# Two-layer mixture kernel: preparing the second layer's factors by a model of the queues, Strassen sums held in PSUM, a plain last w2 product

## The chip, the cores and the metric

The kernel runs on one core of a Trainium2 chip. The metric is device time in microseconds (us), from one launch to its end. TensorE multiplies matrices, VectorE, ScalarE and GpSimd work element by element, SyncE (SP) issues DMAs; each works through its own queue in order and waits there on semaphores. In the profile's rows PE is TensorE, PEld its weight loads, DVE is VectorE, ACT is ScalarE and POOL is GpSimd. Ln is line n of the kernel before.

## The reference

```python
# chunked attention (4 x 8 heads, 576 positions, chunks of 64, 64 wide) gives x, 2304 x 512
scores = scale * np.matmul(q_c, k_c.transpose(0, 1, 2, 4, 3))
...
x = np.ascontiguousarray(attn_out.transpose(0, 2, 1, 3)).reshape(B * S, H * D)
# layer 1: w_a, w_b 512 x 1536, w_out 1536 x 512
a = x @ w_a
b = x @ w_b
x = (a * b @ w_out).astype(np.float32)
# layer 2: 4 experts, w1 512 x 1024, w2 1024 x 512
p = domain_probs / (domain_probs.sum(-1, keepdims=True) + 1e-09)
for e in range(E):
    h = np.maximum(x @ w1[e], 0.0)
    out += p[:, e:e + 1] * (h @ w2[e])
```

## The kernel before, in words

**Numbers and products.** All is computed near float32. A factor is split into a rounded high half (fp32r) and the rest (low half): split_hi is a ScalarE cast (L96), sub_hi a subtraction, on GpSimd by default (L111). A product of two factors is three matmuls (high by high, high by low, low by high) into one PSUM bank of 512 columns; a weight tile is 128x128. add is a VectorE tensor_tensor (L99), add_sb a VectorE scalar_tensor_tensor (L103).

**Strassen.** Tokens come in blocks: block 0 has 256, blocks 1 to 4 have 512 each. From the third of six groups of layer 1 weights (F) on, blocks 1 and 2 are done together by seven half-size products in place of eight, in seq (L621 inside half_mm issues the matmuls; the name A marks this step in the loops). ScalarE copies the first bank (L646), and VectorE forms the four results in SBUF tiles. In layer 2 blocks 1 and 2 (first pass, p = 0) and blocks 3 and 4 (second pass, p = 1) go through the same seq for w1 and through seven products for w2.

**Layer 1.** Attention runs in slots between matmul groups, densest at the start. ab_steps (L508) makes a and b of one block; end_b multiplies them on VectorE, and to_parts splits the product into gh (high) and ag (low, GpSimd). x2_steps (mm3, L461 to L463) multiplies them by w_out and adds into xacc on VectorE, some steps later; the list after says behind which step. The 36 w1 tiles come as float64 and are converted by prep_begin (L140 to L154) and split by prep_end and ent_s, at places written out by hand (put).

**Preparation of the second layer's factors.** prep_ahead is a list of closures that prep takes one by one at fixed steps. A unit is half of one of 16 groups of w1 and w2, one 512 KB raw tile: 32 units. For each there are two split halves, four 256-column Strassen sums in place on VectorE (sums, L103), two more halves, and for each of the four a 512 KB store to DRAM (save, from ScalarE's queue). The tile is loaded from SP's queue (L192) two units ahead. 87 of the 128 halves are made in layer 1, in weight tiles (w), and 41 in layer 2, in tiles of the raw pool (made).

**Layer 2.** The loop over s has 32 steps of w1 (a_steps, group a = s) interleaved, product by product, with the w2 products of the step before (o_step, o = s - 1, L852). a_steps runs seq; on weighs each result by relu and the expert's probability on VectorE (L810) and splits it (part_of_h). t_steps forms the four differences T1 to T4 on GpSimd (L832) and splits them. o_step's seven products go to pairs of PSUM banks (po, two pairs), and VectorE adds each into its y (L99, 1024 columns; ScalarE copies in a pass's first step, L859). In the first pass block 0 rides along: a0_step (24 matmuls of 256 columns) and o0_step (12 matmuls, L926). load_l2 loads the prepared weights from DRAM on SP, in an order written out once. ends forms the four outputs of a pass from the seven y's, on VectorE, 1024 columns each. In the last step t_steps runs on VectorE, and the seven products, ends and the stores follow each other.

Of the kernel before, what the change touches and what calls it, by code (L numbers as in the profile page):

```python
# [22 lines left out]

H_SCALE = 2.0**-112
H_MAX = (1.0 + 0x6FFFFF / 2.0**23) * 2.0**-96


@with_exitstack
def fused_kernel(
# [25 lines left out]
    nc = tc.nc  # L55
# [16 lines left out]
    w_p = ctx.enter_context(tc.tile_pool(name="w", bufs=9))  # L72
    raw_p = ctx.enter_context(tc.tile_pool(name="raw", bufs=4))
# [11 lines left out]
    def psum():  # L85
        return ps_p.tile([P, 512], F32, tag="ps", name="ps")

    def psum_m():
        return psm_p.tile([P, 512], F32, tag="pm", name="pm")
# [72 lines left out]

    def split_w(src, t=None, eng=nc.gpsimd):
# [6 lines left out]
    unsaved = []  # L170

    def save(behind=0):
        while len(unsaved) > behind:
            key, t = unsaved.pop(0)
            saved[key] = tc.dram_tile([P, 2, 512], F32, name="kept" + "_".join(map(str, key)))
            nc.scalar.dma_start(out=saved[key], in_=t.bitcast(F32))
# [5 lines left out]
    def prep_ahead():  # L182

        raw2 = {}
        todo = [(g, i) for g in range(NG2) for i in range(2)]

        def load(n):
            if n < len(todo):
                g, i = todo[n]
                r = raw2[n] = raw_p.tile([P, 1024], F32, tag="raw", name="raw2")  # L190
                src = w2p[g, :, 2 * i : 2 * i + 2, :]
                nc.sync.dma_start(out=r, in_=src.rearrange("p a n -> p (a n)"))  # L192

        def ent(n, k):
            g, i = todo[n]
            save()
            half = raw2[n][:, 512 * (k % 2) :][:, :512]
            t = None
            if "2" in late:
                t = raw_p.tile([P, 2, 512], F32R, tag="raw", name="made")  # L200
            t = split_w(half, t)
            unsaved.append(((g, 4 * i + k), t))
            if k == 3:
                load(n + 2)

        def sums(n):
            q = [raw2[n][:, 256 * x : 256 * x + 256] for x in range(4)]
            a11, a12, a22, a21 = q if todo[n][1] == 0 else (q[0], q[2], q[3], q[1])
            add_sb(a22, a21, a22)
            add_sb(a21, a11, a21, ALU.subtract)  # L210
            add_sb(a11, a22, a11, ALU.subtract)
            add_sb(a12, a12, a11, ALU.subtract)

        yield lambda: (load(0), load(1))
        for n in range(len(todo) + 1):
            if n < len(todo):
                yield from (lambda n=n, k=k: ent(n, k) for k in range(2))
            if n:
                yield from (lambda n=n, k=k: ent(n - 1, k) for k in (2, 3))
            if n < len(todo):  # L220
                yield lambda n=n: sums(n)

    ahead = list(prep_ahead())

    def prep(n=1):
        for _ in range(n):
            if ahead:
                ahead.pop(0)()

    wl = {}  # L230
    l2_loads = [(0, 0, n) for n in (0, 2, 3, 1)]
    for go in range(2 * NG2):
        for n in (0, 4, 2, 7, 5, 3, 6, 1):
            at = divmod(go + (n < 4), NG2)
            if at[0] < 2:
                l2_loads.append((*at, n))

    def load_l2(n=1):
        for _ in range(n):
            if l2_loads:  # L240
                p, g, k = l2_loads.pop(0)
                t = w_tile()
# [247 lines left out]
    def to_parts(g, h, l):  # L490
        split_hi(h, g)
        sub_hi(nc.gpsimd, l, g, h)

    def ab_steps(f, j, i0, nt):
# [21 lines left out]
        def end_b():  # L516
            g = st["g"][:, :n]
            add(g, st[1][:, :n], g, ALU.mult)
            gs[f, j, i0] = (gh_any()[:, :n], ag_tile(F32R)[:, :n])
            to_parts(g, *gs[f, j, i0])  # L520
# [33 lines left out]
    def combos(b11, b21, b12, b22, t_at, eng_b=nc.gpsimd, eng_t=nc.vector):  # L554
# [38 lines left out]
        s3 = [sub(t4, t2, b21)]  # L593
# [36 lines left out]
    def seq(w, t, on, bank=psum_m):  # L630
# [31 lines left out]
        add(t["c22"], pd, t["u3"])  # L662
        out("22", t["c22"])
# [8 lines left out]
        add(t["c12"], pd, t["u2"])  # L672
        flush()
        out("12", t["c12"])
# [68 lines left out]
    def seq_ab(F):  # L743
# [4 lines left out]
        def on_a(name, ap):  # L748
            if name == "11":
                nc.scalar.copy(out=ga["11"], in_=ap)  # L750

        def on_b(name, ap):
            g = ga[name]
            (add if name == "11" else add_sb)(g, ap, g, ALU.mult)
            f, j = 2 * F + (name[0] == "2"), int(name[1])
            gs[f, j, 0] = (gh_tile(name), ag_tile(F32R))
            to_parts(g, *gs[f, j, 0])

        def gen():
# [3 lines left out]
            t |= {"c22": t["m1"], "c12": t["u2"]}  # L763
            yield from seq(lambda x: left(F, 0, x), t, on_a, psum)
            t["m1"] = t["c22"] = gh_tile("22", F32)
            t["u2"] = t["c12"] = gh_tile("12", F32)
# [5 lines left out]

    H = {}
    G = {}
# [5 lines left out]
        ("A12", "B21"),  # L780
        ("S1", "T1"),
        ("S3", "T3"),
        ("S2", "T2"),
# [8 lines left out]
    def part_of_h(a, name, src, eng=nc.gpsimd):  # L792
        pool = late["1" if name in ("B11", "B22") else "2"]
        t = pool.tile([P, 2, 512], F32R, tag="h" + name, name="h" + name, bufs=1)
        H[a, name] = (t[:, 0, :], t[:, 1, :])
        split_hi(t[:, 0, :], src)
        sub_hi(eng, t[:, 1, :], src, t[:, 0, :])

    def a_steps(a):
# [3 lines left out]
        t = {n: late["1"].tile([P, 512], F32, tag=n, name=n, bufs=2) for n in ("m1", "u2", "u3", "g")}  # L803
        t["c22"], t["c12"] = t["m1"], t["u2"]
        prob = pb[p, g // GPE]

        def on(name, src):
            dst = t["g"] if name == "11" else src
            j = int(name[1]) - 1
# [8 lines left out]
            G[a, name] = dst  # L818
            if name != "12":
                part_of_h(a, "B" + name, dst)  # L820

        return steps_of(seq(lambda x: w[x], t, on), 7)

    def t_steps(a, eng):

        g11, g21, g12, g22 = (G[a, n] for n in ("11", "21", "12", "22"))

        def sub(o, x, y):
            if eng is nc.vector:
                add_sb(o, x, y, ALU.subtract)  # L830
            else:
                eng.tensor_tensor(out=o, in0=x, in1=y, op=ALU.subtract)  # L832

        return [
            lambda: (sub(g11, g12, g11), sub(g12, g22, g12)),
            lambda: (part_of_h(a, "T1", g11), sub(g22, g22, g11)),
            lambda: (part_of_h(a, "T3", g12), sub(g21, g22, g21)),
            lambda: part_of_h(a, "T2", g22),
            lambda: part_of_h(a, "T4", g21),
        ]  # L840

    def o_step(o, k, after=None):
# [4 lines left out]
        bh, bl = H.pop((o, part))  # L847
        ps = late["ps"].tile([P, 2, 512], F32, tag="po", name="po")
# [7 lines left out]
        if after is not None:  # L856
            add(y, y, ps, ALU.subtract)
        elif g == 0:
# [9 lines left out]
    def ends(p):  # L868
# [3 lines left out]
        def go(o, x, z, op=ALU.add, at=None):  # L872
            add_sb(y[o], y[x], y[z], op)
            if at:
# [9 lines left out]
            lambda: go("A22", "S3", "A22", ALU.subtract),  # L884
# [439 lines left out]
```

## Time and profile before

| | |
|---|---|
| median of 3 runs | 1315.87 us (1309.72 to 1317.66) |
| the profiled execution | 1309.49 us |
| its span, first to last instruction | 1307.7 us |
| mean granted TensorE clock | 0.979 |
| busy: TensorE, VectorE, GpSimd, ScalarE | 1230.7, 993.0, 889.2, 432.2 us |

A group of rows names a line, an engine, an operation, its tiles as out<-in, and its shapes; behind the bar are the idle time of the engine just before those instructions and what ended it. A row of waits reads: who waited, for whom, microseconds in total, times, longest. Matmuls are pipelined, so the end of a matmul row lies some 0.2 us after the start of the next one.

### The profile page before, as it was taken

The numbers are of one execution on the slowest core, as the hardware profiler recorded it, in microseconds if no ns is written. First come the engines' busy times: TensorE is split into PE (matmuls) and PEld (weight loads), VectorE is DVE, ScalarE is ACT, GpSimd is POOL, SyncE is SP. The second block draws the span as 40 slices with busy tenths as digits, with TensorE's granted clock in tenths as the row PEclk, the third lists the DMA queues.
The fourth block names the chain that finished last, engine by engine and source line by source line (L and its number), as shares of the span: only waits on it lengthen the run. The fifth ranks groups of instructions, "written<-read, shape, count | busy, mean of one in ns | idle before, by whom it ended". The sixth has DMA issues, their size and how long they took to land.

```text
span 1307.7 us, 18028 instructions
## 1 busy us (share of the span) xinstructions
PE 1230.7 (94%) x6674; PEld 1004.6 (77%) x6676; DVE 993.0 (76%) x1247; ACT 432.2 (33%) x785; POOL 889.2 (68%) x669
## 2 busy tenths in 40 slices
PE   8998899889899897999999999999999999999996
PEld 5876678668677776888887878788877888888884
DVE  7856458878686877755888788867788788778778
ACT  4644434433424333334222322222233222222221
POOL 4536567776656756656867776866787777777773
PEclk9999889899899998999999999999999999999998
DMA  8645434444435434266778767855537776676662
GB/s 283 220 138 189 176 130 165 156 161 150 173 128 179 160 129 145 113 221 239 264 253 285 276 248 273 290 176 189 183 129 271 254 247 219 211 246 225 207 213 79
DMA packets 76820, 261.35 MB, mean 200 GB/s; under 512 B 8546, under 2 KB 8618, under 8 KB 76732
## 3 DMA queue, kind: packets, MB, share of 16 engines
q1 hardware_dynamic: 58300, 193.07, 45.0%
q10 hardware_dynamic: 18432, 67.12, 12.7%
q8 instruction: 53, 0.87, 0.3%
q14 instruction: 35, 0.29, 0.1%
HBM read 188.29 MB, written 71.86 MB: 199 GB/s over the span
## 4 chain that ended last, share of the span: by engine, by line
PE 48%; DVE 15%; POOL 3%; issue 2%; ACT 2%; DMA 1%; DVEq 0%; ACTq 0%; POOLq 0%
PE pm L621 19%; PE po L852 18%; PE po L926 3%; DVE raw L103 3%; DVE y L99 3%; PE pm L508 2%; DVE u L810 2%; POOL w L111 1%; DMA raw<-in_w2p_dram 1%; PE ps L461 1%; PE ps L463 1%; PE ps L462 1%; DVE u L99 1%; PE pm L463 1%; PE pm L462 1%
## 5 line engine op out<-in xcount | busy, mean ns | idle before, releaser
L99 DVE TENSOR_TENSOR y<-po,y 128x1024 f32<-128x1024 f32 x209 | 253.8, 1219 | 69.4 <-PE po L852 69.2
L852 PE MATMUL po<-hT,w 128*128 128x512 f32 x768 | 197.8, 393 | 6.1 <-POOL hT L111 4.2
L621 PE MATMUL pm<-cT,w 128*128 128x512 f32 x768 | 195.9, 390 | 0.0
L621 PE MATMUL pm<-cB,w 128*128 128x512 f32 x672 | 175.1, 396 | 15.6 <-ACT ag L646 15.5
L852 PEld LDWEIGHTS po<-hT,w 128*128 128x128 f32 x768 | 144.6, 189 | 39.3 <-POOL hT L111 5.9
L111 POOL TENSOR_TENSOR w<-raw,w 128x512 fp32r<-128x512 f32 x87 | 121.8, 1400 | 77.1 <-ACT w L96 71.8
L621 PEld LDWEIGHTS pm<-cT,w 128*128 128x128 f32 x768 | 143.1, 188 | 29.9
L621 PEld LDWEIGHTS pm<-cB,w 128*128 128x128 f32 x672 | 126.0, 190 | 44.1 <-ACT ag L646 17.2
L852 PE MATMUL po<-hB,w 128*128 128x512 f32 x576 | 150.3, 397 | 7.9 <-DVE y L99 7.4
L852 PEld LDWEIGHTS po<-hB,w 128*128 128x128 f32 x576 | 106.8, 188 | 38.2 <-DVE y L99 14.5
L508 PE MATMUL pm<-xh,w 128*128 128x512 f32 (+1 forms) x576 | 135.8, 357 | 0.0
L103 DVE SCALAR_TENSOR_TENSOR raw<-raw 128x256 f32<-128x256 f32 x128 | 113.2, 885 | 12.2 <-POOL w L111 8.9
L461 PE MATMUL ps<-ag,w 128*128 128x512 f32 (+1 forms) x244 | 95.2, 390 | 23.2 <-POOL ag L111 21.2
L508 PEld LDWEIGHTS pm<-xh,w 128*128 128x128 f32 x576 | 99.7, 190 | 16.6
L111 POOL TENSOR_TENSOR ag<-ag,gh 128x512 fp32r<-128x512 f32 (+1 forms) x61 | 77.2, 1271 | 51.4 <-ACT gh L96 50.0
L99 DVE TENSOR_TENSOR xacc<-ps,xacc 128x512 f32<-128x512 f32 (+1 forms) x112 | 68.0, 628 | 40.8 <-PE ps L463 40.4
L96 ACT CAST w<-raw 128x512 fp32r<-128x512 f32 x87 | 53.9, 620 | 130.7 <-DMA raw<-in_w2p_dram 57.3
L111 POOL TENSOR_TENSOR hT<-u,hT 128x512 fp32r<-128x512 f32 x64 | 94.9, 1483 | 0.0
L463 PE MATMUL ps<-gh,w 128*128 128x512 f32 (+1 forms) x244 | 92.0, 377 | 0.5 <-POOL w L111 0.5
L154 POOL TENSOR_TENSOR t<-t,raw 128x512 int32<-128x512 int32 x36 | 47.5, 1319 | 66.1 <-issue 23.8
L462 PE MATMUL ps<-gh,w 128*128 128x512 f32 (+1 forms) x244 | 92.0, 377 | 0.0
L832 POOL TENSOR_TENSOR u<-m,u 128x512 f32<-128x512 f32 x62 | 82.6, 1331 | 2.4
(141 smaller groups left out, 2342.5 us busy)
## 6 DMA issues: line engine op xcount, KB each, us to landing
w<-kept SPq DMA_DIRECT2D x256, 512.0 KB, 4.6
kept<-w ACTq DMA_DIRECT2D x87, 512.0 KB, 2.6
kept<-made ACTq DMA_DIRECT2D x41, 512.0 KB, 5.9
raw<-in_w1p_dram SPq DMA_DIRECT2D x36, 512.0 KB, 3.7
raw<-in_w2p_dram SPq DMA_DIRECT2D x32, 512.0 KB, 4.5
q<-in_q_dram SPq DMA_DIRECT2D x18, 256.0 KB, 3.8
k<-in_k_dram SPq DMA_DIRECT2D x18, 256.0 KB, 4.2
v<-in_v_dram SPq DMA_DIRECT2D x18, 256.0 KB, 4.1
```

The lines of the kernel that those rows point to most:

```text
L96: nc.scalar.copy(out=dst, in_=src)
L99: nc.vector.tensor_tensor(out=out, in0=in0, in1=in1, op=op)
L103: nc.vector.scalar_tensor_tensor(out=out, in0=in0, scalar=1.0, in1=in1, op0=ALU.mult, op1=op)
L111: eng.tensor_tensor(out=dst, in0=src, in1=hi.bitcast(F32), op=ALU.subtract)
L154: nc.gpsimd.tensor_tensor(out=t.bitcast(I32), in0=t.bitcast(I32), in1=low.bitcast(I32), op=ALU.add)
L461: nc.tensor.matmul(out=ps[:, :n], lhsT=wh, rhs=al, start=(m == 0), stop=False)
L462: nc.tensor.matmul(out=ps[:, :n], lhsT=wh, rhs=ah, start=False, stop=False)
L463: nc.tensor.matmul(out=ps[:, :n], lhsT=wl, rhs=ah, start=False, stop=(m == last))
L508: nc.tensor.matmul(out=st[i][:, :n], lhsT=x, rhs=y, start=m == 0, stop=m == 3 * KD - 1)
L621: nc.tensor.matmul(out=ps, lhsT=x, rhs=y, start=first and kk == 0 and m == 0, stop=kk == 1 and m == 2, skip_group_check=not first,)
L832: eng.tensor_tensor(out=o, in0=x, in1=y, op=ALU.subtract)
L852: nc.tensor.matmul(out=ps[:, d, :], lhsT=x[:, s], rhs=y, start=m == 0, stop=m == 2)
```

## The change

1. Class Plan wraps the program builder: at build time it keeps, for each engine, the time at which its queue would be free, by a duration for each kind of instruction and by when each tile was written and last read. Nothing of it runs on the chip.
2. prep_ahead, prep and save go. prepare turns each unit into Jobs (a load from ScalarE's queue, four casts, four low halves and four sums on GpSimd, four stores); tick, called after most steps, issues those whose engine has room and whose inputs are due by the model, and first the jobs of rank 0 (the layer's own h parts). A unit is begun every 20 us of the model's TensorE time in layer 1, from the fourth span on, and every 14 in layer 2. load_l2 issues what is missing of a tile that it is asked for.
3. Pools: w 9 to 7 tiles plus 3 for made; raw 4 to 2 plus one raw2. load_l2's order of tiles changes.
4. to_parts subtracts on VectorE, and the product stays in its PSUM bank. seq takes A12 B21 sixth, not third, and leaves its results in PSUM. The x2 steps of layer 1 come at steps 6, 8 and 8 on (before 6, 8, 4, 5 and 8).
5. a_steps no longer uses seq: one bank takes four products, and T1 and T3 are formed on VectorE, T2 and T4 on GpSimd. PRODUCTS has a new order; the splits of h are Jobs.
6. The last step's w2 product is four plain products (o_last, 48 matmuls) added to y's on which ends(1) has been run before.

```diff
+class Plan:
...
+    def note(self, name, op, out, ins):
+        t = self.start(name, op, out, ins)
+        if op == "dma_start":
+            self.at[name] = t + 0.36
+            end = t + DMA_US
+        else:
+            us, port = self.cost(name, op, out, ins)
+            end = t + us
...
-    w_p = ctx.enter_context(tc.tile_pool(name="w", bufs=9))
-    raw_p = ctx.enter_context(tc.tile_pool(name="raw", bufs=4))
+    w_p = ctx.enter_context(tc.tile_pool(name="w", bufs=7))
+    raw_p = ctx.enter_context(tc.tile_pool(name="raw", bufs=2))
...
+        if SUMS == "DVE":
+            add_sb(o, y, z, op)
+        else:
+            nc.gpsimd.tensor_tensor(out=o, in0=y, in1=z, op=op)
...
+        def fits(self, now):
+            if not (self.when() and all(j.done for j in self.after)):
+                return False
+            free = max(plan.at[self.q], plan.at["port"] if self.q != "ACT" else 0)
+            if free > now + SLACK[self.rank][self.q] + (hurry() if self.rank else 0):
+                return False
+            return self.ready() <= max(free, now) + EARLY[self.q]
...
     def to_parts(g, h, l):
         split_hi(h, g)
-        sub_hi(nc.gpsimd, l, g, h)
+        add(l, g, h.bitcast(F32), ALU.subtract)
...
-            add(g, st[1][:, :n], g, ALU.mult)
+            b = st[1][:, :n]
+            add(b, b, g, ALU.mult)
...
-        half_mm(pa, w("A12"), c["B21"], first=False)
-        out("11", pa)
-        yield
         pc = psum_m()
         half_mm(pc, w("S3"), c["T3"])
-        flush()
         add(t["u3"], pc, t["u2"])
         yield
         pd = psum_m()
         half_mm(pd, w("S1"), c["T1"])
-        add(t["c22"], pd, t["u3"])
-        out("22", t["c22"])
+        add(pc, pd, t["u3"])
+        out("22", pc)
         yield
         pe = bank()
         half_mm(pe, w("A22"), c["T4"])
-        add(t["u3"], t["u3"], pe, ALU.subtract)
+        add(pe, t["u3"], pe, ALU.subtract)
         flush()
-        out("21", t["u3"])
+        out("21", pe)
+        yield
+        half_mm(pa, w("A12"), c["B21"], first=False)
+        flush()
+        out("11", pa)
...
+            x = psum_m()
+            half_mm(x, w["A11"], c["B11"])
+            nc.scalar.copy(out=t["m1"], in_=x)
+            yield
+            y = psum_m()
+            half_mm(y, w["S1"], c["T1"])
+            nc.scalar.copy(out=t["m5"], in_=y)
+            yield
+            half_mm(x, w["S2"], c["T2"], first=False)
+            nc.scalar.copy(out=t["u2"], in_=x)
+            yield
+            z = psum_m()
+            half_mm(z, w["A12"], c["B21"])
+            add(z, z, t["m1"])
+            weigh(t["g"], z, 0)
+            yield
+            part_of_h(a, "B11", t["g"])
+            half_mm(x, w["S3"], c["T3"], first=False)
+            v = psum_m()
+            add(v, x, t["m5"])
+            weigh(t["m5"], v, 1)
+            yield
+            part_of_h(a, "B22", t["m5"])
+            half_mm(y, w["S4"], c["B22"], first=False)
+            add(y, y, t["u2"])
+            weigh(y, y, 1)
+            yield
+            half_mm(x, w["A22"], c["T4"], first=False)
...
+            add(t["u2"], y, t["g"], ALU.subtract)
+            made_h[a, "B11"].run()
+            add(t["g"], t["m5"], y, ALU.subtract)
+            weigh(t["m1"], x, 0)
...
+                for k in (3, 4, 5, 6):
+                    e[k]()
+                for i, j in ((0, 1), (1, 1), (0, 0), (1, 0)):
+                    o_last(i, j)
+                break
```

## Rows read from the trace of the kernel before

**Rows 1.** The page, first part: busy time, share of the span, instructions.
```profile
PE 1230.7 (94%) x6674; PEld 1004.6 (77%) x6676; DVE 993.0 (76%) x1247; ACT 432.2 (33%) x785; POOL 889.2 (68%) x669
```

**Rows 2.** Windows: length, then busy (instructions) PE PEld DVE ACT POOL, PEclk, DMA.
```profile
75.00:570.00 495.00, 450.03 (x2340) 364.63 (x2339) 352.06 (x475) 192.83 (x346) 317.46 (x233) 0.96 0.44 156
592.86:851.09 258.23, 251.88 (x1201) 207.78 (x1201) 209.94 (x235) 77.56 (x146) 196.18 (x152) 1.00 0.75 265
851.09:950.35 99.26, 99.26 (x482) 83.58 (x481) 74.83 (x81) 22.26 (x42) 68.93 (x50) 1.00 0.54 180
950.35:976.70 26.35, 25.07 (x121) 20.72 (x121) 22.31 (x23) 10.03 (x15) 21.23 (x14) 1.00 0.47 160
979.32:1021.78 42.46, 39.27 (x170) 31.31 (x168) 35.12 (x33) 15.06 (x21) 33.80 (x21) 1.00 0.78 271
1059.67:1078.84 19.17, 19.17 (x85) 15.77 (x84) 15.15 (x16) 4.54 (x8) 14.43 (x11) 1.00 0.73 246
```

**Rows 3.** Waits of TensorE from 75 to 570 us, the four largest.
```profile
PE ps L461 <- POOL ag L111: 20.1, 12, 6.0
PE pm L621 <- ACT ag L646: 15.5, 4, 6.8
PE pm L621 <- DVE gh L99: 3.2, 3, 1.4
PE ps L621 <- DVE xacc L99: 2.6, 3, 1.6
```

**Rows 4.** Windows again: two of layer 1's seven half-clock stretches, and all seven summed.
```profile
344.41:351.23 6.82, 3.80 (x9) 3.02 (x10) 2.42 (x5) 3.25 (x6) 4.97 (x4) 0.50 0.26 107
494.60:501.42 6.82, 3.99 (x9) 3.14 (x10) 4.53 (x8) 3.53 (x7) 2.64 (x4) 0.50 0.21 85
sum 40.92, PE 30.69 PEld 24.37 DVE 21.55 ACT 13.59 POOL 26.14; mean PE 4.38 PEld 3.48 DVE 3.08 ACT 1.94 POOL 3.73
```

**Rows 5.** Timeline, 480 to 500 us: start, length, instruction, [idle before <-releaser].
```profile
484.94 0.62 ACT L96 CAST w<-raw 128x512 fp32r<-128x512 f32 x1 [6.99 <-DMA raw<-in_w2p_dram]
...
497.43 2.93 PE L621 MATMUL pm<-cB,w 128*128 128x512 f32 x6 [6.83 <-ACT ag L646]
```

**Rows 6.** Groups of instructions, shapes apart: busy us, mean ns | idle before.
```profile
L111 POOL TENSOR_TENSOR w<-raw,w 128x512 fp32r<-128x512 f32 x87 | 121.8, 1400 | 77.1 <-ACT w L96 71.8 <-issue 3.7 <-PE ps L463 1.2
L103 DVE SCALAR_TENSOR_TENSOR raw<-raw 128x256 f32<-128x256 f32 x128 | 113.2, 885 | 12.2 <-POOL w L111 8.9
...
L810 DVE SCALAR_TENSOR_TENSOR u<-u,pb 128x512 f32<-128x512 f32 x64 | 68.8, 1075 | 2.2
L111 POOL TENSOR_TENSOR ag<-ag,gh 128x512 fp32r<-128x512 f32 x47 | 65.7, 1405 | 38.5 <-ACT gh L96 37.3 <-PE pm L508 1.0
...
L99 DVE TENSOR_TENSOR ag<-pm,ag 128x512 f32<-128x512 f32 x47 | 32.1, 686 | 18.2 <-PE pm L621 8.1 <-PE pm L508 6.5 <-POOL ag L111 3.2
L96 ACT CAST gh<-ag 128x512 fp32r<-128x512 f32 x47 | 29.1, 620 | 101.4 <-DVE ag L99 80.9 <-DVE ag L103 12.5 <-PE ps L463 7.9
...
L810 DVE SCALAR_TENSOR_TENSOR g<-pm,pb 128x512 f32<-128x512 f32 x32 | 22.1, 691 | 8.4 <-PE pm L621 6.4 <-DMA pb<-probs_n 1.2
...
L103 DVE SCALAR_TENSOR_TENSOR s<-t 128x256 f32<-128x256 f32 x16 | 19.5, 1258 | 0.0
...
L111 POOL TENSOR_TENSOR ag<-ag,gh 128x256 fp32r<-128x256 f32 x14 | 11.5, 824 | 12.9 <-ACT gh L96 12.7
```

**Rows 7.** Waits of TensorE from 592.9 to 1264 us, the largest.
```profile
PE po L852 <- DVE y L99: 7.2, 11, 1.3
```

**Rows 8.** Timeline of the end, from the last w1 product (TensorE) on.
```profile
1279.19 1.52 PE L621 MATMUL pm<-cB,w 128*128 128x512 f32 x6
...
1299.17 3.62 DVE L103 SCALAR_TENSOR_TENSOR y<-y 128x1024 f32<-128x1024 f32 x3
1302.70 1.21 DVE L99 TENSOR_TENSOR y<-y,po 128x1024 f32<-128x1024 f32 x1
```

**Rows 9.** Waits of all engines over the whole span, the longest.
```profile
ACT hB L96 <- DVE m L810: 143.4, 32, 6.4
```

More of the change, by code (lines that the diff above doesn't have):

```diff
@@ L181, in fused_kernel @@
     )
[L182 to L228, printed above, removed]
+    todo = [(g, i) for g in range(NG2) for i in range(2)]
+    raw2 = {}
+    made = {}
+    def raw2_tile(name):
+        return plan.ring("raw2", raw_p.tile([P, 1024], F32, tag="raw2", name=name, bufs=1), 1)
+    def load_raw2(n):
+        g, i = todo[n]
+        raw2[n] = raw2_tile("raw2")
+        src = w2p[g, :, 2 * i : 2 * i + 2, :]
+        nc.scalar.dma_start(out=raw2[n], in_=src.rearrange("p a n -> p (a n)"))
@@ new lines, in written, with over, old, hurry @@
+    def written(tile):
+        return plan.written.get(tile.tensor.name, 0)
+    def over(tile):
+        return max(written(tile), plan.read.get(tile.tensor.name, 0))
+    def old(tag, back):
+        return max([0] + [plan.read.get(x, 0) for x in plan.rings.get(tag, [])[-back:][:1]])
+    begun = [None, 0.0]
+    HUR = 0.04
+    def hurry():
+        late = plan.at["PE"] - begun[1] + pace() * sum(j.rank for j in jobs) / 17
+        return HUR * max(0, late)
+    def prepare(n, first):
+        def fresh():
+            return old("raw", 2) if nxt["prep"] == len(pieces) else old("made", 3)
+        def job(q, go, after, ready):
+            return Job(q, go, after, ready, rank=1)
+        raw = lambda: written(raw2[n])
+        before = job("ACT", lambda: load_raw2(n), first, lambda: old("raw2", 1))
+        his, los = {}, {}
+        stores = []
+        for k in range(4):
+            if k == 2:
+                for x in range(4):
+                    before = job(
+                        SUMS,
+                        lambda x=x: sums2(n, x),
+                        (los[0], los[1]) if x == 0 else (before,),
+                        lambda: over(raw2[n]),
+                    )
+            after = (before, *stores[-1:])
+            his[k] = job("ACT", lambda k=k: hi2(n, k), after, lambda: max(raw(), fresh()))
+            los[k] = job("POOL", lambda k=k: lo2(n, k), (his[k],), lambda k=k: over(made[n, k]))
+            if k % 2:
+                for m in (k - 1, k):
+                    stores.append(
+                        job("ACT", lambda m=m: store2(n, m), (los[m],), lambda m=m: over(made[n, m]))
+                    )
+        return (los[2], los[3], stores[-1])
@@ new lines, in fused_kernel, with tick, pace @@
+    last_raw = [()]
+    def tick():
+        now = plan.at["PE"]
+        if begun[0] is not None and begun[0] < len(todo) and now >= begun[1]:
+            last_raw[0] = prepare(begun[0], last_raw[0])
+            begun[0] += 1
+            begun[1] += pace()
+        while True:
+            j = next((j for r in (0, 1) for j in jobs if j.rank == r and j.fits(now)), None)
+            if j is None:
+                return
+            j.run()
+    def pace():
+        return PACE_2 if "2" in late else PACE_1
@@ L241, in load_l2 @@
                 p, g, k = l2_loads.pop(0)
-                t = w_tile()
+                while (g, k) not in saved:
+                    if not any(j.rank for j in jobs):
+                        last_raw[0] = prepare(begun[0], last_raw[0])
+                        begun[0] += 1
+                    next(j for j in jobs if j.rank).run()
+                t = made_tile() if len(l2_loads) % 10 in (2, 5, 8) else w_tile()
                 nc.sync.dma_start(out=t.bitcast(F32), in_=saved[g, k])
```

356 lines of the change are left out of this document (245 added, 111 removed).

## The prediction

> **What bounds the kernel now.** The page comes first: TensorE is busy 94% of the span, so its matmuls are the floor and only its own lost time can be won [rows 1]. I then cut the span into stages and read how long each takes, how much of it TensorE sits idle, and its granted clock [rows 2]. The cuts of layer 2 lie at starts of the same group of matmuls, one step apart, so each stretch is a whole number of steps. Three readings matter.
>
> A second-pass step without any wait takes 19.17 us; it has 84 matmuls in 14 groups of six, so a group takes 1.37 us and a matmul 0.228 us. A first-pass step, once the preparation is over, takes 99.26/4 = 24.8 us with TensorE never idle: that is its floor. While the preparation still runs beside it ten steps take 258.23 us, 10.1 us over that floor.
>
> Layer 1 (75 to 570 us) is where most is lost: 495.0 - 450.0 = 45.0 us idle at a mean clock of 0.96 [rows 2]. The waits of TensorE there have two large causes: 20.1 us for GpSimd's low half of a gated product (tile ag, line 111) and 15.5 us for ScalarE's copy of the first Strassen product (line 646); the next two come to 3.2 + 2.6 = 5.8 us [rows 3]. The long ones also cost clock: in seven stretches of 3.4 or 6.8 us, all beside such waits, the granted clock is 0.50, the lower level (1.2 GHz); TensorE is busy for 30.69 us of them, work that takes half as long at 2.4 GHz, so 15.3 us more is lost [rows 4]. 45.0 + 15.3 = 60.3 us is all that layer 1 can give.
>
> The timeline shows why those low halves and copies are late: queues run in order, and the preparation stands at fixed places in them. At 484.94 ScalarE has just sat 7.0 us on a cast whose raw w2 tile was still landing; at 497.43 TensorE has waited 6.83 us for a copy issued further down that queue [rows 5]. VectorE's quarter sums are the other blocker: the 128 of them average 885 ns [rows 6], so a block of four holds VectorE 3.5 us, while a PSUM bank waits to be emptied.
>
> **The change part by part.** The sums are made against the profiled execution: span 1307.7 us, 1309.49 us in all.
>
> *Order inside seq and PSUM results.* The product that adds to the first one's bank moves from third to sixth place. ScalarE's copy of that bank therefore has four products to hide behind (4 x 1.37 = 5.5 us) and not one: of the four waits on line 646 (15.5 us, longest 6.8) each shrinks by up to 4.1 us, so at the old lateness at most 2.7 + 1.1 stays, and 12 go. Two stretches at half clock belong to them, at 344 and 494 us, (3.80 + 3.99)/2 = 3.9 us [rows 4]. I take 12 + 4 = 16 us; bounds 0 and 19.
>
> *Low halves of the gated products on VectorE.* The subtraction of 61 tiles leaves GpSimd (1405 ns for 512 columns) and reads PSUM on VectorE; its nearest row is the product from PSUM, 686 ns [rows 6]. It stands right behind the product and the cast, and no longer behind the preparation's GpSimd work. It costs VectorE 61 x 0.69 = 42 us at most, hidden: the 128 sums that leave it held it 113 us. The chain itself cannot vanish: product 0.69, cast 0.62, subtraction 0.69 is 2.0 us, and in the spans before F = 1 only two groups of three matmuls (1.37 us) stand between; I leave 1 us in each of some eight spans, and take 12 of the 20.1 us. Of the other 15.3 - 3.9 = 11.4 us of clock, 8 go with them. Sum 20 us; bounds 6 (only the longest wait of 6.0 goes) and 31.
>
> *Preparation by a model of the queues.* Each unit still has four casts (ScalarE), four low halves (GpSimd) and four stores, and its load now issues from ScalarE's queue and not from SP's. What changes is when: a job is issued if the model sees its inputs there. The four sums go to GpSimd. Nothing here shows them on it: the nearest row is the 256-column subtraction of 824 ns, so 3.3 us a unit and 105 us over 32 units; each lies between half of that (0.4) and the 1.4 us of the 512-column row [rows 6]. GpSimd gives back 61 low halves (some 77 us by the same rows, 47 of 512 columns and 14 of 256) and, in layer 2, two of its four T subtractions a step, so it ends lighter and this hides. The pace, one unit per 20 us from the fourth span on (near 75 us), brings (570 - 75)/20 = 24 of 32 units into layer 1, against 22 now (87 low halves on tile w, four a unit [rows 6]). For the 5.8 us of smaller waits I take 3 us; bounds -4 and 6.
>
> *First pass of layer 2.* VectorE loses a block of four sums (3.5 us) in each of ten steps, and its weighings all read PSUM now: 691 ns for such a row, 1075 for one from two SBUF tiles [rows 6]. TensorE's largest waits in layer 2 before the end are on VectorE's y additions, 7.2 us in 11 times [rows 7]. I take 8 of the 10.1 us; bounds 0 and 10. What would be late next is GpSimd: nine instructions a step at 1.4 us (12.6) and a unit (4 x 1.4 + 3.3 = 8.9 us) per 14 us of pace make 28 us in a 24.8 us step, so the pace is not met; the eight units left need 8 x 8.9 = 71 us of a spare 12.2 us a step, six steps, where today's ten carry the preparation.
>
> *From pass to pass.* The step at 950 us takes 26.35 us for 24.8, and the two at 979 take 42.46 for 38.3 [rows 2]: 1.5 + 4.1 us, on T factors from a GpSimd behind VectorE's wide sums. Two T subtractions a step now read PSUM on VectorE. I take 2 us; bounds 0 and 5.6.
>
> *New order of a_steps.* One bank takes four products, and three are read out between: two ScalarE copies and one VectorE sum. Three groups (4.1 us) lie between a bank's product and the next into it, a copy takes about what a cast does (0.62), so it hides unless ScalarE is held over 3.5 us. T1 is needed five groups (6.9 us) after the last product, and takes two VectorE instructions, a cast and a low half, some 3.4 us. In the second pass I see nothing late and leave 19.17 us a step. For banks held longer, by two instructions in place of one, I subtract 3 us; bounds 0 and -10.
>
> *Plain last step.* 48 matmuls for 42 cost 6 x 0.228 = 1.4 us on the path. Now the last w1 product ends at 1279.19 + 1.37 = 1280.6, and 27.1 us follow [rows 8]. After: at that point VectorE has 1.2 us to finish, then a weighing (0.69), two low halves (1.38), one y addition (1.21) and five sums (1.21 each, a third of the row at 1299.17, 6.05): 10.5 us. The first plain product's addition ends at 11.7 and frees the bank for the third; the last two products take 2 x 2.74, the last half's addition 0.9, and from the last addition to the end I keep today's 1307.7 - 1303.9 = 3.8 us: 21.9 us. Won: 5 us; bounds 1 (VectorE half again as slow) and 9 (TensorE never waits).
>
> Sum: 16 + 20 + 3 + 8 + 2 - 3 + 5 = 51 us, of which 39 in layer 1. Span 1256.7, that execution 1258.5. It lies 6.4 us under the median of the runs (1315.87); carried over, the forecast is 1265 us. At the lower bounds 3 - 10 = -7 us, at the upper 81 us.
>
> **The rivals.** *The waits stay, with another owner.* The 36 w1 tiles keep their fixed places: casts, sums (1258 ns for 256 columns [rows 6]) and low halves of their own in the same queues. For it: each such sum takes nearly twice as long as a 512-column one from PSUM (686). Against: the cast that blocked ScalarE for 7.0 us is a w2 one [rows 5]. Then layer 1 gives 12 (half its clock share included), the first pass 5, the rest 3: 20 us, 1296 us.
>
> The row of two SBUF inputs against one from PSUM (1075 and 691 ns) fits the Trainium skill, "SBUF — State Buffer", section "Who interferes with whom": VectorE with two SBUF inputs contends with a GpSimd instruction that reads SBUF, an exclusive lock that the first holds throughout. By that rule the sums moved to GpSimd would slow each w1 sum that is left, which is this rival; the product and low half that read PSUM would be free of it, which is the forecast.
>
> *The model is wrong about room.* Jobs pile up and are forced when a load asks for their tile: a unit is then 8.9 us of GpSimd in a burst, and a burst late by itself in two places in layer 1 and two in layer 2 costs 4 x 8.9 = 36 us: 1301 us, and with a few more of them no change, some 1312. For: one raw buffer instead of a shared four. Against: units are issued far ahead of need.
>
> *Slower: ScalarE's copies gate TensorE.* Its queue is in order, and today hB casts hold it up to 6.4 us, 143.4 us in 32 times, without harm since one copy a step is all that TensorE waits for [rows 9]. Now each step has three copies, two of them only three groups ahead of the next product into the same bank. If a cast stands 6.4 us in front of one, TensorE waits 6.4 - 3.5 = 2.9 us; in 31 steps 90 us, which is 39 more than won: 1355 us. It decides from 51/31 = 1.6 us a step. Against it: a cast is a job now, issued when its source is due.
>
> **How the numbers follow.** The forecast (a gain of 32 to 78 us) has 0.62, the waits with another owner 0.18, the wrong model 0.13, the slower one 0.07. A measurement tells about 1% (13 us) from no change. The first two cases are faster by more; of the third a quarter lies over 13 us (0.03) and the rest within (0.10); of the slower one 0.02 stays within. So 0.83 faster, 0.12 within, 0.05 slower. The range goes from 1238 (the upper bounds but for 3 us) to 1306, which takes in the second rival and a part of the third; the forecast's own is 1238 to 1284.
>
> **What would show it.** Right: layer 1 some 39 us shorter, with no wait over 2 us on line 646's copy and none on GpSimd's ag; at most three stretches at half clock there; first-pass steps at 24.8 us from the first on; second-pass steps still 19.17; 22 us behind the last w1 product; 48 matmuls of the plain form. Wrong: waits of TensorE in layer 2 on ScalarE's copies, second-pass steps over 19.5 us, or layer 1 still over 480 us with waits whose releaser is a w1 instruction.

## The result, and the profile after

The changed kernel takes 1252.28 us (median of 4 runs, 1248.34 to 1254.37) against 1315.84 of the kernel before in the same session (1309.72 to 1317.66): a ratio of 0.952, 95% interval 0.948 to 0.956. The forecast was 1265 us, in a range of 1238 to 1306.

The profiled execution took 1248.34 us, with a span of 1246.5 us and a mean granted clock of 0.996. It is the fastest of the four, 3.9 us under their median, and two executions of nearly the same program differ in single stages (a_tail below issues the same instructions up to its last step, and its layer 2 begins 2.3 us later), so figures of one stage hold to some 2 to 4 us. The page's first part answers to [rows 1]. (All calls go through one helper now, so every row is on line 41; tiles and shapes tell the groups apart.)

```profile
PE 1208.0 (97%) x6682; PEld 999.1 (80%) x6682; DVE 851.7 (68%) x1174; ACT 474.1 (38%) x858; POOL 800.6 (64%) x669
```

TensorE is busy 22.7 us less with no fewer matmuls: 15.3 us of that is the half clock of layer 1 [rows 4], which is gone. VectorE is 141 us lighter and GpSimd 89, ScalarE 42 heavier. The windows of the stages answer to [rows 2], with the same columns: layer 1, three steps without loss, step 4, four later first-pass steps, the second and third step of the second pass, a plain second-pass step, and the tail behind the last w1 product.

```profile
75.00:515.50 440.50, 429.40 (x2339) 355.86 (x2338) 291.60 (x443) 185.41 (x339) 271.82 (x230) 1.00 0.42 147
532.81:607.25 74.44, 74.44 (x362) 62.68 (x361) 38.95 (x50) 33.85 (x57) 60.08 (x55) 1.00 0.80 286
607.25:637.18 29.93, 26.45 (x122) 21.81 (x121) 18.76 (x23) 11.60 (x21) 24.78 (x23) 0.94 0.77 287
787.20:886.46 99.26, 99.26 (x483) 83.60 (x481) 67.46 (x82) 31.92 (x59) 72.37 (x58) 1.00 0.67 241
933.81:973.96 40.15, 38.59 (x170) 31.46 (x168) 32.08 (x33) 18.37 (x28) 26.35 (x18) 1.00 0.89 315
1031.48:1050.65 19.17, 19.17 (x85) 15.77 (x84) 14.26 (x17) 5.80 (x11) 11.46 (x9) 1.00 0.68 222
1221.85:1246.49 24.64, 14.92 (x55) 10.85 (x53) 15.44 (x16) 0.75 (x2) 0.00 (x0) 0.93 0.22 85
```

In layer 1 TensorE was idle 45.0 us at a mean clock of 0.96; now it is idle 11.1 us at 1.00. Its waits there answer to [rows 3]:

```profile
PE ps L41 <- DVE ag L41: 4.9, 6, 2.1
PE pm L41 <- DVE pm L41: 4.8, 3, 2.8
PE ps L41 <- ACT aT L41: 1.3, 1, 1.3
```

Neither GpSimd's low half (20.1 us before) nor the copy of the first bank (15.5) is left. Cutting both traces at the first w1 matmul of each step of layer 2 gives a ledger of the 61.2 us between the two spans:

| stage | before, us | after, us | gained | forecast |
|---|---|---|---|---|
| start to layer 2 | 569.0 | 515.5 | 53.5 | 39 |
| step 0 | 15.3 | 17.3 | -1.9 | 0 |
| first pass, steps 1 to 11 | 283.1 | 279.2 | 3.9 | 8 - 3 |
| steps 12 to 18, of which 15 to 18 lead from pass to pass | 165.2 | 161.9 | 3.3 | 2 |
| tail behind the last w1 product | 27.1 | 24.6 | 2.5 | 5 |

The other second-pass steps take 19.17 us in both. Where the steps of layer 2 lose is read from its timeline, here in step 4 (start, length, instruction, idle before and releaser):

```profile
611.98 0.62 ACT L41 CAST made<-raw 128x512 fp32r<-128x512 f32 x1 [2.71 <-DMA kept<-made]
...
614.53 0.62 ACT L41 CAST made<-raw 128x512 fp32r<-128x512 f32 x1 [1.93 <-DMA kept<-made]
...
615.84 1.07 ACT L41 COPY m<-pm 128x512 f32<-128x512 f32 x2
...
616.48 0.80 PE L41 MATMUL pm<-cT,w 128*128 128x512 f32 x1 [3.48 <-ACT m L41]
```

Read it from below: TensorE waits 3.48 us for ScalarE's copy of a bank; the copy stands behind two casts of the preparation, and each cast waited for a store of the tile that it overwrites. The same took 0.8 us in step 9. In step 0 a copy came 1.6 us late behind another job of the preparation: the issue of a store, which stood 1.5 us in ScalarE's queue until GpSimd had made the low half to be stored. That is 6.0 us in three places. The groups that the prediction had priced from neighbouring rows [rows 6]:

```profile
L41 POOL TENSOR_TENSOR made<-raw,made 128x512 fp32r<-128x512 f32 x128 | 168.8, 1335 | 84.5 <-ACT made L41 84.5
L41 POOL TENSOR_TENSOR raw<-raw 128x256 f32<-128x256 f32 x128 | 100.9, 789 | 9.9
...
L41 DVE TENSOR_TENSOR ag<-pm,gh 128x512 fp32r<-128x512 f32 x43 | 29.7, 692 | 32.7 <-ACT gh L41 32.7
...
L41 DVE SCALAR_TENSOR_TENSOR s<-t 128x256 f32<-128x256 f32 x16 | 9.3, 622 | 0.0
```

The sums cost 789 ns on GpSimd (824 taken), a low half from PSUM 692 ns on VectorE (690 taken). The last row was not foreseen: the w1 sums, untouched by the change, take 622 ns and not 1258.

### The profile page after: what moved, and what is told of

Its sections match the earlier page's. It is cut to its first block, busy times and chain, and to the rows that moved or that the text cites. A ratio compares the mean times of both kernels' runs of the same rounds, so it can differ in the third digit from the quotient of the medians.

```text
span 1246.5 us, 18136 instructions
## 1 busy us (share of the span) xinstructions
PE 1208.0 (97%) x6682; PEld 999.1 (80%) x6682; DVE 851.7 (68%) x1174; ACT 474.1 (38%) x858; POOL 800.6 (64%) x669
## 4 chain that ended last, share of the span: by engine, by line
PE 45%; DMA 2%; DVE 2%; POOL 2%; issue 1%; ACT 0%; ACTq 0%; POOLq 0%; DVEq 0%
PE po L41 23%; PE pm L41 22%; DVE y L41 1%; DMA raw<-in_w2p_dram 1%; DMA kept<-made 1%; DMA w<-kept 1%; POOL made L41 1%; POOL hT L41 0%; DVE pm L41 0%; POOL m L41 0%; POOL hB L41 0%; ACT made L41 0%; POOL raw L41 0%; DVE cT L41 0%; DVE g L41 0%
## 5 line engine op out<-in xcount | busy, mean ns | idle before, releaser
L41 POOL TENSOR_TENSOR made<-raw,made 128x512 fp32r<-128x512 f32 x128 | 168.8, 1335 | 84.5 <-ACT made L41 84.5
L41 PE MATMUL pm<-cB,w 128*128 128x512 f32 (+1 forms) x768 | 190.7, 384 | 0.0
L41 PE MATMUL ps<-gh,w 128*128 128x512 f32 (+1 forms) x488 | 137.8, 365 | 0.0
L41 PE MATMUL po<-hT,w 128*128 128x512 f32 x492 | 125.6, 389 | 1.0 <-DVE hT L41 1.0
L41 PEld LDWEIGHTS po<-hT,w 128*128 128x128 f32 x492 | 92.6, 188 | 20.9 <-DVE hT L41 1.4
L41 POOL TENSOR_TENSOR raw<-raw 128x256 f32<-128x256 f32 x128 | 100.9, 789 | 9.9
L41 ACT CAST made<-raw 128x512 fp32r<-128x512 f32 x128 | 75.9, 621 | 71.2 <-DMA raw<-in_w2p_dram 39.7
L41 PEld LDWEIGHTS ps<-gh,w 128*128 128x128 f32 x488 | 87.9, 188 | 14.7
L41 POOL TENSOR_TENSOR hB<-m,hB 128x512 fp32r<-128x512 f32 x63 | 81.6, 1295 | 26.4 <-ACT hB L41 26.4
L41 POOL TENSOR_TENSOR hT<-m,hT 128x512 fp32r<-128x512 f32 x62 | 81.1, 1309 | 16.0 <-ACT hT L41 14.8
```

Of the source, the lines that this page charges most:

```text
L41: return call(*args, **kw)
```

## The experiments

Two theories stood against each other. The *parts* theory is the prediction's: the new order (16), the low halves (20) and the placement (3) each give their own share of layer 1. The *placement* theory: it is the preparation, standing in the queues, that makes things late, and the local edits only pay once it is out of the way. Kernels whose label begins with b are the kernel before plus an edit, those with a the changed kernel with an edit. The latter also have a few lines that issue what is left of the preparation before step 13, when its buffers are wanted; in the changed kernel as it is these issue nothing. In the b kernels the A steps keep their results in SBUF tiles, so in b_lo and b_both 31 of the 47 wide low halves read PSUM and 16 do not.

**b_lo: the low halves alone.**

```diff
-        sub_hi(nc.gpsimd, l, g, h)
+        add(l, g, h.bitcast(F32), ALU.subtract)
...
-            add(g, st[1][:, :n], g, ALU.mult)
+            b = st[1][:, :n]
+            add(b, b, g, ALU.mult)
```

> The kernel before with one part of the change: the low halves of the gated products are subtracted on VectorE, in the ab steps from the product kept in PSUM. Parts theory (each part of the change takes away its own waits, as in the ledger): the 20 us of GpSimd's ag waits go but for about 8, with half of their clock, so some 1300 us (ratio 0.988). Placement theory (the preparation's fixed places in the queues make all of layer 1's waits, and only taking it out of the way helps): the wait moves to ScalarE's casts or VectorE's sums, ratio 0.997 to 1.005.

1312.1 us, ratio 0.998 (0.996 to 0.999). TensorE's two largest waits from 75 to 570 us:

```profile
PE pm L622 <- ACT ag L647: 17.6, 4, 6.4
PE ps L461 <- DVE ag L99: 14.8, 9, 4.2
```

The 20.1 us on GpSimd's ag became 14.8 us on VectorE's. The wait changed owner.

**b_seq: the order alone** (A12 B21 sixth in layer 1's seq, not third).

```diff
+        if third:
+            half_mm(pa, w("A12"), c["B21"], first=False)
+            out("11", pa)
+            yield
...
+        if not third:
+            half_mm(pa, w("A12"), c["B21"], first=False)
+            flush()
+            out("11", pa)
+            yield
...
-            yield from seq(lambda x: left(F, 0, x), t, on_a, psum)
+            yield from seq(lambda x: left(F, 0, x), t, on_a, psum, False)
```

> The kernel before with one part of the change: in layer 1 the product that adds to the first bank is sixth and not third (results stay in SBUF). Parts theory: the 15.5 us of waits on ScalarE's copy go but for 3, with 4 us of clock, some 1300 us (ratio 0.988). Placement theory: the copy comes as late as before and the next consumer waits instead, ratio 0.995 to 1.0.

1315.97 us, ratio 1.003 (1.000 to 1.006), no gain at all. The waits on the copy are gone, as the prediction's reasoning says, and their time is on GpSimd's low half (37.0 us, 20.1 before):

```profile
PE ps L461 <- POOL ag L111: 37.0, 20, 5.6
```

**b_both: the two together.**

> The kernel before with both local edits at once: low halves of the gated products on VectorE, and the A12 product sixth in seq. Theory (the preparation's fixed places hold the queues, and the local edits only move the wait to another owner): layer 2 still begins at 563 to 576 us, 1303 to 1320 us in all, TensorE's waits in layer 1 now on VectorE and ScalarE. Rival (the two edits help each other, and make most of layer 1's gain without the model): layer 2 begins near 535 us, 1280 us in all.

1301.15 us, ratio 0.990 (0.988 to 0.992). Layer 2 begins at 558.8 us, 10.2 earlier; but steps 2 to 11 take 25.3 to 26.3 us, as in the kernel before, with short waits on VectorE's y. Somewhat better than the placement theory said, far from the rival's 535: the two help each other by some 13 us, and the rest has another source. Layer 1's window and its largest wait:

```profile
75.00:558.80 483.80, 444.77 (x2340) 362.88 (x2339) 353.03 (x531) 190.35 (x345) 243.01 (x177) 0.98 0.45 160
```
```profile
PE ps L461 <- DVE ag L99: 18.4, 13, 4.5
```

**b_noprep: the kernel before without the preparation's engine work.** It leaves out the casts, low halves and sums of the w2 units; each raw tile is stored as it is.

```diff
-            t = split_w(half, t)
+            t = raw2[n].rearrange("p (a n) -> p a n", a=2)
...
-            add_sb(a22, a21, a22)
...
+            pass
```

> The kernel before with the preparation's 128 casts, 128 low halves and 128 sums left out; each raw tile is loaded and stored four times as it is, so loads and stores stay and the later products use unprepared factors. Theory (that work, standing at fixed places in the queues, is what makes TensorE wait in layer 1): waits on the low half of the gated product and on the copy of the first bank fall from 35.6 to under 10 us, no more than two stretches at half clock, layer 2 begins at 515 to 530 us, first-pass steps 24.8 to 25.0 us, 1255 to 1270 us in all. Rival (the w1 tiles' fixed places own the waits): layer 2 begins after 550 us, and the gain is under 25 us.

1251.68 us, ratio 0.953 (0.951 to 0.955). Layer 2 begins at 520.95 us, and the first-pass steps 1 to 15 take 24.8 each. The two waits fall from 35.6 to 13.6 us, not under 10 as the theory had it; two stretches at half clock are left in layer 1, within what it allowed. The waits:

```profile
PE ps L455 <- POOL ag L111: 10.7, 7, 5.2
PE pm L615 <- ACT ag L640: 2.9, 3, 1.7
```

That is the strongest evidence for the placement theory: with its order and its low halves as they were, the kernel before loses 48 us in layer 1 to the preparation, and the rival in which the w1 tiles' fixed places own the waits falls. The changed kernel does all of that work and is as fast as this one without it, so it is not the amount of work alone. One thing stays mixed in: without casts and low halves the preparation also claims no weight tiles (pool w) in layer 1, and what that is worth was not tried.

**a_lopool: the low halves back on GpSimd** in the changed kernel, their product in SBUF again.

```diff
-        add(l, g, h.bitcast(F32), ALU.subtract)
+        sub_hi(nc.gpsimd, l, g, h)
```

> The kernel after with the low halves of the gated products back on GpSimd, from a product in SBUF. Parts theory: GpSimd's ag waits are back, 15 to 20 us more than after (1268 us). Placement theory: with the preparation placed by the model GpSimd is free when they come, at most 4 us more.

1274.13 us, ratio 0.968 (0.966 to 0.971): 22 us slower than the changed kernel, 17.1 of them by the start of layer 2 (532.6 us); 6.5 fall in step 13 (31.3 us), where what is left of the preparation is issued at once. The low halves on VectorE, worth 0.2% alone, are worth 22 us here. So in the changed kernel it is the parts theory's figure (15 to 20 us) that comes, and the placement theory's (at most 4) that fails. The wait, and the w1 sums:

```profile
PE ps L41 <- POOL ag L41: 17.7, 9, 4.4
```
```profile
L41 DVE SCALAR_TENSOR_TENSOR s<-t 128x256 f32<-128x256 f32 x16 | 17.9, 1157 | 0.0
```

**a_seqold: the A12 product back in third place.**

> The kernel after with the old place (third) of the product that adds to the first bank in layer 1's seq. Parts theory: some 10 us more than after, with waits of TensorE on ScalarE's copy in the four A steps. Placement theory: ScalarE is no longer held by the preparation when the copy is due, at most 3 us more.

1255.91 us, ratio 0.955 (0.953 to 0.957), layer 2 at 521.6 us: 3.6 us by the medians, with overlapping intervals, and 2.2 us of waits on the copy. The order is worth a few us at most, nearer to the placement theory (at most 3) than to the parts theory (some 10).

**a_table: jobs by a timetable, not by room.** A unit's 17 jobs come one each 0.8 us, issued when due, whatever stands in their queue.

```diff
+        mine = [j for j in jobs if j.rank][-17:]
+        for i, j in enumerate(mine):
+            j.due = begun[1] + pace() / 20 * (i and 5 + 0.8 * i)
...
+                j = next((j for j in jobs if j.rank), None)
+                if j and not (now >= j.due and all(x.done for x in j.after)):
+                    j = None
```

> The kernel after with the preparation's 17 jobs of a unit issued by a timetable (one every 0.8 us of the pace, the first cast 5.8 us after the load), whatever the queues hold; the layer's own h parts are still issued by the model. If the model's choice of the moment is what counts: 20 to 40 us more than after, with waits on ag and on ScalarE's copies back in layer 1. If it is enough that the jobs come singly and evenly, with the sums off VectorE: at most 8 us more.

1446.1 us, ratio 1.102 (1.099 to 1.105). Layer 1 alone is 205 us longer, with the clock at 0.86:

```profile
75.00:720.50 645.50, 490.65 (x2344) 393.00 (x2343) 284.11 (x445) 218.41 (x396) 376.12 (x343) 0.86 0.45 159
```

But this was no clean comparison. All 32 units came in layer 1, one each 18 us, while the changed kernel began 18, one each 25.5 us (counted from the starts of the casts): it asks for a unit every 20 us, and its model does not grant that. So the moment and the rate were mixed up, which the next run takes apart.

**a_tab28: the same timetable at the rate that the changed kernel really had** (a unit every 28 us in layer 1, every 21 in layer 2).

```diff
-    PACE_1 = 20
-    PACE_2 = 14
+    PACE_1 = 28
+    PACE_2 = 21
```

> The changed kernel with the preparation's jobs by a timetable instead of by room: one unit begun every 28 us of the model's TensorE time in layer 1 and every 21 us in layer 2, its 16 further jobs from 7.0 us on and 1.12 us apart, at the next place in the program once due, whatever stands in the queue; so some 17 or 18 units in layer 1, as many as the changed kernel makes. Theory (the moment chosen by room in the queues is what counts): layer 2 begins 25 us or more later than 515.5, past 540 us, 1275 us or more in all, with TensorE waits on low halves and products of over 2 us. Rival (only the slower pace counts: 18 units for 22): layer 2 begins at 512 to 525 us, 1248 to 1262 us in all.

1261.71 us, ratio 0.960 (0.958 to 0.962), with 17 units before layer 2, which begins at 521.95: 6.4 us later than in the changed kernel. Two first-pass steps (31.3 and 31.7 us) lose 13.4 more, while steps 4 and 9 lose nothing:

```profile
75.00:521.90 446.90, 434.64 (x2350) 359.33 (x2349) 281.81 (x445) 185.73 (x339) 262.54 (x225) 0.99 0.40 140
538.18:601.22 63.04, 54.69 (x243) 43.13 (x242) 25.20 (x35) 26.27 (x44) 46.53 (x43) 0.95 0.74 260
```

My theory that the moment is what counts failed by its own number (past 540 us). The rival's numbers came, just: at a rate that the queues bear, a blind timetable of single jobs is 9.4 us worse than the model; at a rate that they don't, 194 us. These two runs differ in the pace alone, so as far as they show, what the model does above all is to hold the preparation back.

**a_sumdve: the sums back on VectorE.**

```diff
-    SUMS = "POOL"
+    SUMS = "DVE"
```

> The kernel after with the quarter sums on VectorE (still placed by the model, against VectorE's queue). If moving them off VectorE counts: 10 to 20 us more, from TensorE's waits on VectorE's ag in layer 1 and on y in the first pass (10 us there in the kernel before). If the model finds room for them on VectorE too: within 4 us of after.

1279.87 us, ratio 0.975 (0.973 to 0.978), and yet layer 2 begins at 512.7, 2.8 us earlier, with 16 units made before it, and the first-pass steps 1 to 12 take 24.8 or 24.9. The whole loss is in step 13 (67.1 us for 24.8): the units were not done, and what was left was issued at once.

```profile
PE pm L41 <- ACT m L41: 40.7, 1, 40.7
```
```profile
L41 DVE SCALAR_TENSOR_TENSOR raw<-raw 128x256 f32<-128x256 f32 x128 | 75.0, 586 | 45.9 <-POOL made L41 45.0
```

So the sums on GpSimd are not what shortens layer 1; they make the units come in time.

**a_dma8: the model takes a transfer as 8 us, not 6** (DMA_US).

> The kernel after with the model's time of a DMA at 8 us and not 6 (loads and stores). If ScalarE's casts held by a store that lands later than modelled cause the 3.5 us wait on ScalarE's copy in the first pass (with its half-clock stretch): first-pass steps all at 24.8 us and 3 to 6 us less. If units then come later and more of them are forced into layer 2: 3 to 10 us more.

1310.44 us, ratio 0.997 (0.996 to 0.999). The first-pass steps 1 to 12 stay within 24.8 to 24.9 us: the casts wait 0.9 us for stores in the whole run, for 19.8 in the changed kernel, so step 4's loss is the store landing later than planned. But only 15 units are made before layer 2, which begins at 523.1 us, and the price is the same as above, 60.7 us at step 13, far over the 3 to 10 us that were expected of units coming late:

```profile
PE pm L41 <- ACT m L41: 60.7, 1, 60.7
```

**a_tail: the last step's sums set between its plain products.**

```diff
-                for k in (3, 4, 5, 6):
-                    e[k]()
-                for i, j in ((0, 1), (1, 1), (0, 0), (1, 0)):
-                    o_last(i, j)
+                for ks, i, j in (((3,), 0, 1), ((4, 5), 1, 1), ((6,), 0, 0), ((), 1, 0)):
+                    for k in ks:
+                        e[k]()
+                    o_last(i, j)
```

> The kernel after with the last step's sums on VectorE issued between the plain products' additions, each just before the addition that needs it. By the queue of VectorE: the first addition ends some 3.6 us earlier, the wait of 3.74 us of TensorE for its bank goes, and the last addition ends some 16 us after the last w1 product and not 21.1: 5 us less (1247 us). If VectorE's total work sets the end and not the bank: no change within 1 us.

1249.43 us, ratio 0.951 (0.948 to 0.954), the fastest version run, though its interval overlaps the changed kernel's. From the last w1 product (1228.23) to the end (1249.4) it takes 21.2 us, for 24.6. In its timeline the sums come two by two and the wait of 3.74 us has become one of 0.41, with 0.69 and 1.22 later; no stretch at half clock falls before the last matmul. (In this execution step 9 loses 5.0 us, where the changed kernel's lost 1.2: the same instructions, another execution.)

```profile
1233.07 2.48 DVE L41 SCALAR_TENSOR_TENSOR y<-y 128x1024 f32<-128x1024 f32 x2
...
1236.93 3.03 PE L41 MATMUL po<-hB,w 128*128 128x512 f32 x12 [0.41 <-DVE y L41]
```

**a_best: an attempt to keep the tail and win steps 4 and 9.**

```diff
-DMA_US = 6.0
+DMA_US = 6.5
...
-    HUR = 0.04
+    HUR = 0.06
...
-        R_FROM = 3
+        R_FROM = 0
```

> The changed kernel with four edits: units begun from the first span on instead of the fourth, a transfer taken as 6.5 us instead of 6.0, the bonus for late jobs raised by half, and the last step's sums set between its plain products. Theory (the first pass's two losses of 5.1 and 1.1 us come from stores that land later than the model says, and units that start earlier leave room to wait for them): steps 4 and 9 of the first pass at 24.8 to 25.3 us, 21 to 22 us from the last w1 product to the end, layer 2 begins at 513 to 520 us, 1242 to 1248 us in all. Rival (any change of the model's figures only deals the waits to other places): losses of 5 us or more at other steps or in layer 1, 1249 to 1258 us.

1268.07 us, ratio 0.965 (0.963 to 0.967): slower than the changed kernel, and than the rival said. Steps 2 to 12 take 24.8 us each and the tail 21.3, as hoped, but layer 2 begins at 540.9 us, with 20 units made before it. Its largest wait in layer 1 is new, and the timeline of GpSimd shows what it is:

```profile
PE pm L41 <- POOL S L41: 13.6, 4, 5.5
```
```profile
260.25 2.54 POOL L41 TENSOR_TENSOR made<-raw,made 128x512 fp32r<-128x512 f32 x2 [0.37 <-ACT made L41]
262.87 3.58 POOL L41 TENSOR_TENSOR raw<-raw 128x256 f32<-128x256 f32 x4
266.40 1.26 POOL L41 TENSOR_TENSOR S<-s,S 128x512 fp32r<-128x512 f32 x1
```

Two low halves and four sums of the preparation, 6.1 us, stand in front of the low half of a w1 factor that TensorE waits for until 267.7 us. Three figures of the planning were changed at once, so which of them let the jobs in is open.

## Why the prediction was right, and where its steps failed

**Size and sign.** 51 us were forecast and 61 came in the profiled executions. The excess lies in layer 1, 53.5 for 39; all else came to 7.8 for 12. The bound of 60.3 us that idle time and half clock set there [rows 2, 4] held.

**Order, 16 us; low halves, 20; placement, 3.** The sum came near by luck: its division was wrong. I had priced each edit by the wait that it removes, and added. By themselves they are worth nothing (b_seq +0.3%, b_lo -0.2%), because the next late thing takes the wait; together 1.0%; in the changed kernel, undone, 4 and 22 us. Taken in this order, of layer 1's 53.5 us, 10.2 come with the two local edits (b_both), 6.4 with the model's choice of the moment (a_tab28 against after), and the 36.9 between b_both and a_tab28 with the rest: single jobs in place of blocks, 17 units in place of 22, the A steps' results left in PSUM, and the x2 steps' and loads' new places. Another order divides otherwise: with all the rest in, the low halves alone are 17.1 (a_lopool). The sums' move is not among them (a_sumdve). How that rest divides was not tried. The term "placement 3 us" is the one that failed, where up to 48 us of layer 1 hung on the preparation (b_noprep), and the timeline that I had read [rows 5] named the cause.

**The pace, 24 units in layer 1 and an end near step 7.** Wrong: 18 units, and an end in step 12 (the kernel before ends in step 11). The arithmetic took the pace asked for as the pace granted. ScalarE's casts of the preparation show what holds a unit back, the load of the one raw tile, and the store of the tile to be overwritten:

```profile
L41 ACT CAST made<-raw 128x512 fp32r<-128x512 f32 x128 | 75.9, 621 | 71.2 <-DMA raw<-in_w2p_dram 39.7 <-DMA kept<-made 19.8 <-POOL raw L41 9.7
```

I had counted engine time per unit (8.9 us) and no chain through its buffers. That this chain sets the pace is borne out in part by a_dma8: with transfers taken as longer by the model, 15 units come. GpSimd's and VectorE's load counts too, for a_sumdve has 16.

**First pass, 8, less 3 for new waits.** 3.9 us came, 2.0 with step 0. The floor of 24.8 us was right and most steps reach it; the waits that the last rival described, ScalarE's copies behind a cast, are there, and were named as a sign of being wrong: 6.0 us in three places and not 90 in 31, since they need a job of the preparation that waits in front of the copy. The model's fixed 6 us for a transfer is too short there, though 8 us cost far more elsewhere (a_dma8).

**Pass to pass, 2.** 3.3 us came: T factors no longer delay steps 16 and 17, and a wait of 1.6 us for a load (w<-kept) at 960 us gives some back.

**Tail, 5.** 2.5 us came. The bank was to be free 11.7 us behind the last w1 product; it was after 12.0 (the first of the two additions at 1232.61 takes 1.22 us, and 1233.83 - 1221.85 = 12.0). What failed is the rest:

```profile
1226.69 6.01 DVE L41 SCALAR_TENSOR_TENSOR y<-y 128x1024 f32<-128x1024 f32 x5
...
1232.61 2.35 DVE L41 TENSOR_TENSOR y<-po,y 128x1024 f32<-128x1024 f32 x2
...
1233.88 5.93 PE L41 MATMUL po<-hB,w 128*128 128x512 f32 x18 [3.74 <-DVE y L41]
...
1240.60 1.66 PE L41 MATMUL po<-hB,w 128*128 128x512 f32 x6 [0.78 <-DVE y L41]
```

The sum had TensorE run at full speed from there on, 2 x 2.74 us. The granted clock right behind that wait is 0.50, the lower level (1.2 GHz), and 18 matmuls take 5.93 us where 4.1 would do; another wait of 0.78 follows. In layer 1 I had priced waits with their clock, here not:

```profile
1233.77:1237.18 3.41, 3.29 (x8) 2.62 (x9) 1.19 (x2) 0.00 (x0) 0.00 (x0) 0.50 0.74 286
```

**The rivals.** "The waits stay, with another owner" is what happens to each local edit alone, but its cause, the w1 tiles, was not it (b_noprep). "The model is wrong about room" shows up only where its figures are changed: a_sumdve and a_dma8 lose 42 and 63 us in one forced burst.

## What to carry to other kernels

Price a removed wait only together with what is late next in the same queue: an edit that removes a largest wait can be worth nothing alone (b_lo) and 22 us once the background work is placed otherwise (a_lopool). To find out whether background work is the cause, leave it out once (here 64 us in one run) before moving the foreground about. Background work is issued first of all at a rate that its buffers can bear (9.4 us lost against 194); a margin for its transfers that makes it late costs more than it saves (a_dma8); a wait on the path is priced with the clock that TensorE may lose behind it.

## What the runs showed of the hardware

The 16 w1 sums are VectorE instructions with two SBUF inputs of 256 columns, the same in all kernels. They take 1258 ns before, 1144 in b_noprep and 1157 in a_lopool, where GpSimd makes the low halves of the gated products; they take 718 in b_lo, 720 in b_both, 763 in a_tab28, 839 in a_table and 622 in the changed kernel, where VectorE makes them. The preparation's sums show the same: 885 ns on VectorE before [rows 6], 783 in b_both, 586 in a_sumdve. So a good part of what such an instruction costs is GpSimd beside it. The single instructions show it best. In the kernel before, the only two of the 16 that ran with nothing on GpSimd beside them took 0.41 us each; the two at 454.17 us, beside three low halves on GpSimd, took 1.51 each:

```profile
413.37 0.75 DVE L103 SCALAR_TENSOR_TENSOR s<-t 128x256 f32<-128x256 f32 x2
...
453.67 4.62 POOL L111 TENSOR_TENSOR ag<-ag,gh 128x512 fp32r<-128x512 f32 x3
...
454.17 2.95 DVE L103 SCALAR_TENSOR_TENSOR s<-t 128x256 f32<-128x256 f32 x2
```

The Trainium skill, "SBUF — State Buffer", section "Who interferes with whom", says that a VectorE instruction with two SBUF inputs contends with a GpSimd instruction that reads SBUF; these rows agree. The prediction feared from this rule that sums moved to GpSimd would slow the w1 sums that are left; they became twice as fast. Most of that comes with the gated low halves leaving GpSimd, which alone gives 718 ns (b_lo). What the rest depends on is open: it is not the model as such, for with the same model a_seqold has 829.
